# A fused attention and routed feed-forward kernel: the order of the second part's products, its end, and its first fillers

## The chip, the core and the metric

The kernel runs on one core of a Trainium2 chip. The metric is device time in microseconds (us), the median over runs. A core has five engines that run side by side and wait for each other through semaphores: TensorE (PE, matrix products; it writes only to PSUM), VectorE (DVE), ScalarE (ACT), GpSimd (POOL) and SyncE (SP, which issues DMAs; POOL and ACT issue some too). SBUF holds operands, 128 partitions wide; PSUM has eight banks of 512 fp32 values in each partition. In the profile PE has two rows: matmuls, and the loads of their stationary operand (PEld).

## What is computed

Attention first: 8 batches, 8 heads, 512 local and 32 global tokens of width 64, with a band mask for local tokens and full rows for global ones. Its output, 4352 tokens of width 512, goes to a layer of 8 experts whose weights P come from a normalisation repeated eight times over rows and columns:

```python
x = np.ascontiguousarray(attn_out.transpose(0, 2, 1, 3)).reshape(B * S, H * D)
...
for e in range(E):
    h = np.maximum(x @ w1[e], 0.0)      # 4352x512 @ 512x1024
    ye = h @ w2[e]                      # 4352x1024 @ 1024x512
    out += P[:, e:e + 1] * ye
```

Every expert sees every token. The products are by far most of the work.

## The kernel before

The instruction order on each engine is the order in which the Python code emits them (`manual_schedule`); nothing reorders it later. Waits are added where two engines touch the same tile.

The first part computes attention, and beside it experts 0 and 1 in the plain way: `p_l1` makes one 128-row piece of h (four matmuls), `p_l2` one 128-token piece of the output (eight matmuls). What of these is left over when attention ends stands in the list `tail`; some of it runs during the normalisation, and 13 pieces are still there when the second part starts: three long ones (eight matmuls of 512 columns), eight short ones (four of 256 columns), two long ones. The list of short and long ones matters since a long piece needs all short ones before it.

The second part does experts 2 to 7 in two passes over the tokens, with seven products in the place of eight per 2x2 block matrix (a Strassen-like form, whose sums of operands are made by DVE and POOL). Two kinds of objects do it:

- A `Slot`, called a block here, is a 128-wide piece of h for 1024 tokens: products `m1`, `m2`, `m4`, `m6`, `m5`, `m7`, `m3`, each two matmuls of 512 columns (L895; for the 128-column block of the global tokens each is eight matmuls of 128 columns). It works in three PSUM banks: `pa`, `pc` and `pb`. ACT copies `pa` to `pc` after `m1` (L907), takes relu of `pc` after `m2` (L911) and of `pa` after `m4` (L915), and copies `pa` to SBUF after `m6` (L920) and after `m7` (L929). DVE makes the other two quarters of h with a combined add and relu on `pb` (L899): `c22` after `m7`, and another after `m3`. `m4` writes over `pa` once L929 has read it; `m3` adds to `pb` once `c22` has read it.
- A `Unit` is the second layer for 256 tokens: `m1`, `m7`, `m2`, `m6`, `m4`, `m5`, `m3`, each four matmuls of 256 columns (L800), all in one PSUM tile `z` of two banks from the pool `ps_z`, which has two such tiles. ACT copies within `z` after `m1` (L814) and `m6` (L821). DVE (L834; for expert 2 ACT, L839 and L854) reads `z` into the output accumulator three times: `r2` and `r7` after `m5`, `r1` after `m3`. `sums` (L796) are the four operand sums that DVE makes for a unit.

`run_slot(a, jobs)` weaves them. In one call are at hand the new block `a`, the block of the call before `p`, the unit of the call before `x`, and a new unit `y` from a list. `a.m3`, `a.m4` are left to the next call, and so are `m4`, `m5`, `m3` of `y`. `jobs` are loads of the next weights, token sums, and additions of stored results of experts 0 and 1 (`stored_add`, DVE, L755; loads on SP, L747). In the first calls there is no unit yet and `fill` puts leftover pieces between the products; they take the `z` tiles of `ps_z`.

After the last call, `run_slot(None)` finishes the last block and unit, and `plain` does the last four units as plain products: per 128 tokens eight matmuls of 512 columns (L866) into a `z` tile, then one DVE addition (L869) and a store on SP.

Calls are slots in what follows; there are 102 of them, the first beginning at 363.6 us.

Of the kernel before, what the change touches and what calls it, by code (L numbers as in the profile page):

```python
# [23 lines left out]
def kernel(  # L24
# [28 lines left out]
    FT = F // P  # L53
# [636 lines left out]
    with tc.tile_pool(name="tpool", bufs=2) as tpool, \  # L690
# [68 lines left out]
        def store(m, c, eng):  # L759
            if m < B:  # L760
                r0 = S * m + Sg + P * c
                eng.dma_start(out=out[r0 : r0 + P, :], in_=ogs[m][:, c, :])
            else:
                for b in range(4 * c, 4 * c + 4):
                    eng.dma_start(out=out[S * b : S * b + Sg, :], in_=ogs[m][W * (b % 4) : W * (b % 4 + 1), c, :])
# [15 lines left out]
        class Unit:  # L781
# [21 lines left out]
            def w(self, i, j):  # L803
                return w2s[self.k][:, HF * i : HF * (i + 1), H2 * j : H2 * (j + 1)]
# [52 lines left out]
                if self.e == E - 1:  # L857
                    store(self.m, self.c[0], nc.sync)

        def plain(u, last):  # L860
            order = sorted(range(FT), key=lambda fk: (fk % HF == HF - 1, fk))
            for j in range(2):
                for d0, d1 in ((0, H2), (H2, 3 * P), (3 * P, D)) if last and j else ((0, D),):
                    z = ps_mm.tile([P, D], FP32, tag="mm", name="zq") if d0 else ps_z.tile([P, D], FP32, tag="z", name="zp")
                    for n, fk in enumerate(order):
                        nc.tensor.matmul(z[:, d0:d1], u.a[2 * j + fk // HF][:, fk % HF, :], work["last"][:, fk, d0:d1],  # L866
                                         start=(n == 0), stop=(n == FT - 1), skip_group_check=True)
                    o = u.o(j)[:, d0:d1]
                    nc.vector.scalar_tensor_tensor(out=o, in0=z[:, d0:d1], scalar=u.p[j], in1=o, op0=ALU.mult, op1=ALU.add)  # L869
                store(u.m, u.c[j], nc.sync)  # L870
# [67 lines left out]
        units, state = [], dict(slot=None, unit=None)  # L938

        def run_slot(a, jobs=()):  # L940
            p, x = state["slot"], state["unit"]
            y = units.pop(0) if units else None

            def do(who, *what):
                for w in what:
                    if who is not None:
                        getattr(who, w)()

            def fill(n):
                for _ in range(min(n, len(tail)) if a is not None else 0):  # L950
                    tail.pop(0)[1](pool=ps_z, tag="z")

            do(a, "m1")
            some = -(-len(tail) // (HF - a.f)) if tail and a is not None else 0
            if x is None:
                fill(1)
            if a is not None and p is None:
                fill(some)
            do(x, "m4", "m5", "r2", "r7")
            if x is None:  # L960
                do(p, "m4", "m3")
            do(a, "m2")
            if x is not None:
                do(p, "m4", "m3")
            do(y, "sums", "m1")
            do(a, "m6")
            do(x, "m3", "r1")
            do(a, "m5")
            if y is None:
                fill(some - 1)  # L970
            do(y, "m7", "m2", "m6")
            do(a, "m7")
            for j in jobs:
                j()
            do(a, "c22")
            state["slot"], state["unit"] = a, y
# [30 lines left out]
        for k, (pas, e) in enumerate(stages):  # L1007
# [3 lines left out]
            n = len(slots)  # L1011
# [24 lines left out]
            for (q, f), js in zip(slots, jobs):  # L1036
                if k == 0 and q == 1 and f == 0:
                    hset.append([hpool.tile([P, FT, 512], FP16, tag="hT", name="hs") for _ in range(2)])
                run_slot(Slot(k, q, f, hset[q % 2] if q < NQ else hg), js)
                if q == NQ or f == HF - 1:  # L1040
                    push(k, q)
        final, units = units, []
        run_slot(None)
        for i, u in enumerate(final):
            plain(u, i == len(final) - 1)


# [28 lines left out]
```

## Time and profile before

| what | us |
|---|---|
| median of 3 runs | 1017.83 (1014.74 to 1019.41) |
| the profiled execution, its own time | 1014.45 |
| its span | 1012.7 |
| PE busy | 994.9 |
| DVE busy | 778.5 |
| ACT busy | 632.9 |
| POOL busy | 300.6 |

The granted TensorE clock has a mean of 0.996. The span runs from the first to the last instruction of the program; the time of the execution lies some 2 us above it. The ends of matmuls are modelled in a profile of this kind, so that rows of PE overlap: for PE the starts are what to read. In a timeline each row is a start, a length, an engine and line, the operation, what it writes and reads, their shapes, how many like it follow each other (x), and in brackets the idle time before it and what ended that. In the chain of waits each row is a start, a length, and what the end of the program hung on then.

### The profile page before, as it was taken

The numbers are of one execution on the slowest core, as the hardware profiler recorded it, in microseconds if no ns is written. First come the engines' busy times: TensorE is split into PE (matmuls) and PEld (weight loads), VectorE is DVE, ScalarE is ACT, GpSimd is POOL, SyncE is SP. The second block draws the span as 40 slices with busy tenths as digits, with TensorE's granted clock in tenths as the row PEclk, the third lists the DMA queues.
The fourth block names the chain that finished last, engine by engine and source line by source line (L and its number), as shares of the span: only waits on it lengthen the run. The fifth ranks groups of instructions, "written<-read, shape, count | busy, mean of one in ns | idle before, by whom it ended". The sixth has DMA issues, their size and how long they took to land.

```text
span 1012.7 us, 22301 instructions
## 1 busy us (share of the span) xinstructions
PE 994.9 (98%) x8788; PEld 644.5 (64%) x8788; DVE 778.5 (77%) x1889; ACT 632.9 (62%) x1342; POOL 300.6 (30%) x366
## 2 busy tenths in 40 slices
PE   7899999999999999999999999999999999999997
PEld 4656566656565555666666666676767676766764
DVE  7866666666664664889999888997889999888885
ACT  5877777777774566765555555557765555555551
POOL 9648877887760112111111111111111111100000
PEclk8999999999999999999999999999999999999999
DMA  9999999999852297554443333565664533123043
GB/s 169 180 165 197 226 220 208 203 194 228 208 150 84 90 254 167 156 146 115 115 115 74 73 73 74 126 196 138 161 149 119 115 75 86 47 66 74 1 105 125
DMA packets 135882, 138.42 MB, mean 137 GB/s; under 512 B 54432, under 2 KB 107872, under 8 KB 133728
## 3 DMA queue, kind: packets, MB, share of 16 engines
q0 software_dynamic: 105696, 87.32, 49.1%
q1 hardware_dynamic: 29520, 49.34, 15.0%
q8 instruction: 69, 1.13, 0.5%
q10 hardware_dynamic: 560, 0.33, 0.1%
q14 instruction: 37, 0.30, 0.1%
HBM read 144.20 MB, written 39.58 MB: 181 GB/s over the span
## 4 chain that ended last, share of the span: by engine, by line
PE 94%; DVE 3%; ACT 1%; issue 1%; DMA 0%; ACTq 0%; DVEq 0%
PE z L800 29%; PE pa L895 17%; PE ph L467 12%; PE py L481 11%; PE pb L895 9%; PE pc L895 5%; PE po L384 2%; PE zp L866 1%; PE sc L331 1%; PE ptw L350 1%; PE pk L299 1%; DVE ms L338 1%; PE po L428 1%; DVE Pl L347 1%; PE tgx L360 1%; PE pq L299 1%
## 5 line engine op out<-in xcount | busy, mean ns | idle before, releaser
L800 PEld LDWEIGHTS <-hs 128*128 128x128 f16 x2264 | 220.7, 98 | 92.8 <-issue 1.1
L800 PE MATMUL z<-w2e,hs 128*128 128x256 f16 x1304 | 195.6, 273 | 0.9 <-DVE oy L834 0.9
L800 PE MATMUL z<-v,hs 128*128 128x256 f16 x960 | 144.0, 273 | 0.0
L467 PE MATMUL ph<-xT,w1e 128*128 128x512 f16 (+1 forms) x576 | 129.6, 367 | 2.1 <-DVE lg L456 1.4
L481 PE MATMUL py<-w2e,hT 128*128 128x512 f16 x544 | 128.2, 379 | 0.4 <-DVE hT L472 0.4
L821 ACT COPY z<-z 128x256 f32<-128x256 f32 x98 | 35.0, 357 | 142.0 <-PE z L800 142.0
L895 PEld LDWEIGHTS <-w1e 128*128 128x128 f16 x960 | 86.5, 97 | 57.5 <-issue 1.3
L895 PE MATMUL pa<-t,s 128*128 128x512 f16 x384 | 114.2, 379 | 0.2 <-ACT s L920 0.2
L716 POOL DMA_DIRECT2D w1e<-in_moe_w_dram x24 | 17.4, 732 | 306.2 <-PE pa L895 229.9
L341 ACT ACTIVATE Pu<-ms,mx 128x160 f16<-128x160 f32 x256 | 92.3, 424 | 22.9 <-DVE mx L338 20.2
L834 DVE SCALAR_TENSOR_TENSOR oy<-z,lg,oy 128x512 f32<-128x512 f32 x128 | 95.8, 749 | 7.4 <-ACT oy L839 5.2
L796 DVE TENSOR_TENSOR hs<-hs 128x512 f16<-128x512 f16 x224 | 94.9, 423 | 8.2
L338 DVE CUSTOM_DVE_ANT_0 ms<-sc,mask 128x160 f32<-128x160 f32 x256 | 69.9, 320 | 36.7 <-PE sc L333 34.5
L899 DVE CUSTOM_DVE_ANT_0 hx<-pb,s 128x512 f16<-128x512 f32 x96 | 65.9, 686 | 40.0 <-ACT s L929 31.8
L716 POOL DMA_DIRECT2D w2e<-in_moe_w_dram x24 | 19.8, 830 | 242.7 <-PE z L800 212.4
L911 ACT ACTIVATE hs<-pc 128x512 f16<-128x512 f32 x96 | 57.2, 596 | 52.7 <-PE pc L895 52.6
L467 PEld LDWEIGHTS <-w1e 128*128 128x128 f16 x576 | 53.9, 98 | 52.6 <-issue 2.9
L899 DVE CUSTOM_DVE_ANT_0 hs<-pb,s 128x512 f16<-128x512 f32 x96 | 65.8, 686 | 27.3 <-ACT s L929 26.9
L895 PEld LDWEIGHTS <-s 128*128 128x128 f16 x720 | 65.6, 98 | 29.9 <-issue 1.8
L481 PEld LDWEIGHTS <-hT 128*128 128x128 f16 x544 | 50.0, 98 | 51.8 <-issue 0.5
L472 DVE TENSOR_SCALAR hT<-ph 128x512 f16<-128x512 f32 x58 | 40.1, 692 | 47.7 <-PE ph L467 46.4
L929 ACT COPY s<-pa 128x512 f32<-128x512 f32 x102 | 59.8, 586 | 12.3 <-PE pa L895 1.1
(196 smaller groups left out, 1971.4 us busy)
## 6 DMA issues: line engine op xcount, KB each, us to landing
ys<-yd SPq DMA_DIRECT2D x68, 256.0 KB, 3.4
yd<-yst SPq DMA_DIRECT2D x16, 1024.0 KB, 5.6
pw<-in_moe_w_dram POOLq DMA_DIRECT2D x24, 512.0 KB, 10.3
kept<-psum POOLq DMA_DIRECT2D x24, 512.0 KB, 4.7
s<-kept POOLq DMA_DIRECT2D x12, 768.0 KB, 9.2
v<-kept POOLq DMA_DIRECT2D x12, 768.0 KB, 8.8
w1e<-in_moe_w_dram POOLq DMA_DIRECT2D x12, 512.0 KB, 5.3
w2e<-in_moe_w_dram POOLq DMA_DIRECT2D x12, 512.0 KB, 6.6
```

Source lines behind the costliest of these rows:

```text
L338: nc.vector.tensor_tensor_reduce(out=ms[:, ii, :], in0=sc[:, SW * ii : SW * (ii + 1)], in1=mask[:, mi, :], scale=-scale, scalar=BIG, op0=A ...
L341: nc.scalar.activation(out=d["Pu"][:, i, :], in_=ms[:, ii, :], func=AF.Exp, scale=-1.0, bias=d["mx"][:, i : i + 1])
L467: nc.tensor.matmul(ph[:, 0:n], wts[e][0][:, dk, P * fm : P * (fm + 1)], xT[:, dk, c0 : c0 + n], start=(dk == 0), stop=(dk == DP - 1))
L472: nc.vector.tensor_scalar(out=hT[:, fm, 0:n], in0=ph[:, 0:n], scalar1=0.0, scalar2=None, op0=ALU.max)
L481: nc.tensor.matmul(py, hT[:, fk, P * c : P * (c + 1)], wts[e][1][:, fk, :], start=(fk == 0), stop=(fk == FT - 1))
L796: nc.vector.tensor_tensor(out=o, in0=x, in1=y, op=op)
L800: nc.tensor.matmul(o, lhs[:, fk, :], rhs[:, fk, :], start=(first and fk == 0), stop=(fk == HF - 1), skip_group_check=True)
L834: nc.vector.scalar_tensor_tensor(out=o, in0=z, scalar=p, in1=o, op0=ALU.mult, op1=ALU.add)
L895: nc.tensor.matmul(o, lhs[:, dk, P * f : P * (f + 1)], rhs[:, dk], start=(first and n == 0 and dk == 0), stop=(dk == HD - 1), skip_group_c ...
L899: nc.vector._custom_dve(TENSOR_ADD_SAT, out=self.to(i, j), in0=self.of(ps), in1=self.of(s), s0=BIG, s1=0.0)
L911: nc.scalar.activation(out=self.to(0, 0), in_=self.of(self.pc), func=AF.Relu)
L929: nc.scalar.copy(out=self.pre3, in_=self.pa)
```

## The change

Three edits.

1. In `run_slot`, the old block's `m4` is emitted right after the old unit's products, ahead of the new block's `m2`; it stood between the new block's `m2` and the old block's `m3`. (Where there is no old unit, `m4` and `m3` both stood ahead of `m2`, and still do.)
2. In the first slot, two leftover pieces stand between `m1` and `m2` in place of five, and the count for the rest of the slot is lowered by one. Over the four slots that have pieces, their numbers go from 8, 2, 2, 1 to 4, 3, 3, 3.
3. `run_slot(None)` is written out: the last unit's `m4`, `m5`, `r2`, then the last block's `m4`, `m3`, then `r7`. The last unit's `m3` and `r1` are handed to `plain`, which emits them after six of the eight matmuls of its first product.

```diff
-        def plain(u, last):
+        def plain(u, last, between=()):
             order = sorted(range(FT), key=lambda fk: (fk % HF == HF - 1, fk))
...
                     for n, fk in enumerate(order):
+                        if n == FT - 2 and j == 0:
+                            for f in between:
+                                f()
                         nc.tensor.matmul(z[:, d0:d1], u.a[2 * j + fk // HF][:, fk % HF, :], work["last"][:, fk, d0:d1],
...
             if x is None:
                 fill(1)
             if a is not None and p is None:
-                fill(some)
+                fill(1)
+                some -= 1
             do(x, "m4", "m5", "r2", "r7")
+            do(p, "m4")
             if x is None:
-                do(p, "m4", "m3")
+                do(p, "m3")
             do(a, "m2")
             if x is not None:
-                do(p, "m4", "m3")
+                do(p, "m3")
...
         final, units = units, []
-        run_slot(None)
+        p, x = state["slot"], state["unit"]
+        for w in (x.m4, x.m5, x.r2, p.m4, p.m3, x.r7):
+            w()
         for i, u in enumerate(final):
-            plain(u, i == len(final) - 1)
+            plain(u, i == len(final) - 1, (x.m3, x.r1) if i == 0 else ())
```

## The prediction

> **What bounds the kernel now.** I read the page first, then the busy time by stretch, the chain of waits, and the timeline of one steady slot, of the first slots and of the end.
>
> ```profile
> span 1012.7 us, 22301 instructions
> PE 994.9 (98%) x8788; PEld 644.5 (64%) x8788; DVE 778.5 (77%) x1889; ACT 632.9 (62%) x1342; POOL 300.6 (30%) x366
> ```
> ```profile
> 500.00:550.00 50.00, 50.00 (x344) 33.38 (x342) 46.26 (x82) 28.14 (x57) 5.66 (x8) 1.00 0.47 112
> ```
>
> TensorE (PE) sets the pace; in this stretch of the second part it is busy 50.00 of 50.00 us at a granted clock of 1.00, VectorE (DVE) 46.26, ScalarE (ACT) 28.14. But a PE row's length is not the time it takes from its successor: in the timeline below, two matmuls last 0.59 and the next pair starts 0.43 later. A stall shorter than that overlap is invisible as idle time, so I go by starts.
>
> ```profile
> 984.35 0.59 PE L895 MATMUL pa<-t,s 128*128 128x512 f16 x2
> 984.78 0.59 PE L895 MATMUL pa<-xT,w1e 128*128 128x512 f16 x2
> 985.22 0.60 PE L800 MATMUL z<-v,hx 128*128 128x256 f16 x4
> 985.65 0.60 PE L800 MATMUL z<-w2e,hx 128*128 128x256 f16 x4
> 986.16 0.59 PE L895 MATMUL pc<-xT,w1e 128*128 128x512 f16 x2
> 986.59 0.59 PE L895 MATMUL pa<-t,w1e 128*128 128x512 f16 x2
> 987.02 0.59 PE L895 MATMUL pb<-xT,s 128*128 128x512 f16 x2
> 987.46 0.60 PE L800 MATMUL z<-w2e,hs 128*128 128x256 f16 x4
> 987.89 0.59 PE L895 MATMUL pa<-t,s 128*128 128x512 f16 x2
> 988.32 0.60 PE L800 MATMUL z<-w2e,hs 128*128 128x256 f16 x4
> 988.76 0.59 PE L895 MATMUL pb<-xT,w1e 128*128 128x512 f16 x2
> ```
> ```profile
> 985.04 0.59 ACT L929 COPY s<-pa 128x512 f32<-128x512 f32 x1
> 985.52 0.59 ACT L907 COPY pc<-pa 128x512 f32<-128x512 f32 x1
> ```
> ```profile
> 985.66 0.69 DVE L899 CUSTOM_DVE_ANT_0 hs<-pb,s 128x512 f16<-128x512 f32 x1 [1.01 <-ACT s L929]
> 986.29 1.54 DVE L834 SCALAR_TENSOR_TENSOR oy<-z,lg,oy 128x512 f32<-128x512 f32 x2
> 987.74 0.68 DVE L899 CUSTOM_DVE_ANT_0 hs<-pb,s 128x512 f16<-128x512 f32 x1
> ```
>
> This is a slot, PE's rows first, then ACT's and DVE's: old block's m7 at 984.35, new block's m1 at 984.78, old unit's m4 and m5 at 985.22 and 985.65, new block's m2 at 986.16, old block's m4 and m3 at 986.59 and 987.02. Products follow each other after 0.43 to 0.44, except m2: 0.51 after m5. It waits for the copy of pa into pc (L907), which ends at 985.52 + 0.59 = 986.11; 0.05 later m2 starts. The copy is late because it stands behind L929, the copy of m7.
>
> ```profile
> 451.45 0.45 PE pc L895 x2
> ...
> 457.54 0.50 PE pc L895 x2
> ```
> ```profile
> 405.74 1.31 PE z L800 x12
> ...
> 989.36 1.31 PE z L800 x12
> ```
>
> The chain of waits shows the same as 0.50 (elsewhere 0.45) for a pair that takes 0.43. Between the two z rows lie 95 slots in 583.62 us, 6.143 each. A slot at full rate is 28 matmuls of 256 columns at 1.31/12 = 0.1092 and 14 of 512 at 0.2156 (the mean spacing of the unstalled ones), 6.075; times 95 is 577.1, and the six slots of the 128-column block take some 0.6 more. That leaves 5.9 us of stall. Counted start by start, 62 slots lose 0.075, five 0.060, 27 lose 0.020 and one 0.369: 5.89, all ahead of m2.
>
> [...] Taken instead at its word, the busy row of 50.00 would leave nothing to win in this stretch and the sum below would be 0.9 us.
>
> **Part 1, old block's m4 ahead of new block's m2.** Nothing is added on any engine; PE's order becomes m1, m4, m5 (unit), m4 (block), m2, m3. Take m7 as zero. The block's m4 would start at 1.74 (985.22 + 2 × 0.435 - 984.35). It overwrites pa, so it needs L929, which ends at 985.63, or 1.28 (1.32 with the handover): 0.4 to spare. m2 comes at 2.17 and needs L907, ready at 1.81: 0.36 to spare. So the stall goes. What is late next: m3 of the old block needs c22 (the DVE row at 985.66, ending 986.35, 2.00), and would come at 2.60. The new block's m5 needs pb's last reading (987.74 + 0.68 = 988.42, 4.07) and would come at 4.34 instead of 4.41: the least margin, 0.2. The sums for the new unit's m7, which follows m5, stand behind that same DVE row, the first ending 0.42 or so after it: some 0.3 to spare. ACT reads pa before pc instead of after; pc's relu ends some 0.4 later, and the next use of its output is a slot away. If a cover fails, its late part costs up to 95 × 0.075 again. The DVE needs 46.26/50 × 6.15 = 5.69 a slot, under 6.08, so it doesn't become the pace. Gain taken: 5.9; bounds 0 (another wait takes the place everywhere) and 5.9 (no more stall than this).
>
> The moved product's first matmul now carries a wait on ACT of its own (m2's wait, on a later copy, covered it before): 99 more waits in the built program. The unit's m4 (985.22) carries such a wait too, on an ACT copy that is done by then, and starts 0.44 after its predecessor. I take nothing; the bounds are 0 and, by the one handover that shows (986.11 to 986.16), 0.05 each, 5 us.
>
> **Part 2, leftover pieces spread.**
>
> ```profile
> 370.31 0.60 PE L467 MATMUL ph<-xT,w1e 128*128 128x256 f16 x4 [0.24 <-ACT yst L484]
> ```
> ```profile
> 379.16 0.59 PE L895 MATMUL pa<-t,w1e 128*128 128x512 f16 x2
> 379.86 0.38 PE L895 MATMUL pb<-xT,s 128*128 128x512 f16 x1
> ```
> ```profile
> 387.27 0.59 PE L895 MATMUL pa<-t,s 128*128 128x512 f16 x2
> 387.79 0.59 PE L895 MATMUL pb<-xT,w1e 128*128 128x512 f16 x2
> 388.60 0.38 PE L895 MATMUL pa<-t,s 128*128 128x512 f16 x1 [0.22 <-ACT s L920]
> ```
> ```profile
> 379.62 1.45 POOL L716 DMA_DIRECT2D w1e<-in_moe_w_dram  x2 [21.10 <-PE ph L467]
> ```
>
> Thirteen pieces fill four slots: before 8, 2, 2, 1, after 4, 3, 3, 3; none is added. By starts this region loses 2.1 us. Two short pieces behind three long ones wait for their bank (0.40 and 0.20); after, one short piece follows one long one and the rest come two by two with m7 and m1 between, so these 0.6 go. In the fourth slot m7 waits for its pa copy at 388.60: 0.81 after m5 instead of 0.43, 0.38 lost; after, two long pieces stand there, and it goes. But the fourth slot had a long piece between m1 and m4 that hid c22; now a short one stands there as in the third, where m3 came 0.70 after m4 (379.86 against 379.16), 0.27 lost: that is new. Some 1.1 of waits of 0.08 to 0.3 in the four slots and the first of the units stays. Gain 0.98 - 0.27 = 0.7; bounds 0 and 1.0.
>
> The next weights on POOL's queue (379.62) wait for the last short piece, which moves from the third slot to the fourth, some 3 us later. They are read from the next stage on, four slots of 6.1 after the fourth, so they have over 20 us. The store of the last leftover group goes out a few us later on SP, behind the same loads as before; the accumulator that takes its buffer is first written three slots on. I cost both at nothing; without that cover each would cost its delay, 2 to 4 us once.
>
> **Part 3, the end.**
>
> ```profile
> 992.55 0.59 PE L895 MATMUL pb<-xT,s 128*128 128x512 f16 x2
> 994.00 0.60 PE L800 MATMUL z<-w2e,hs 128*128 128x256 f16 x4 [0.85 <-DVE oy L834]
> 994.43 0.81 PE L866 MATMUL zp<-w2e,hs 128*128 128x512 f16 x3
> ```
> ```profile
> 991.81 0.69 DVE L899 CUSTOM_DVE_ANT_0 hs<-pb,s 128x512 f16<-128x512 f32 x1 [1.01 <-ACT s L929]
> 992.41 1.53 DVE L834 SCALAR_TENSOR_TENSOR oy<-z,lg,oy 128x512 f32<-128x512 f32 x2
> 993.86 0.68 DVE L899 CUSTOM_DVE_ANT_0 hs<-pb,s 128x512 f16<-128x512 f32 x1
> 994.63 0.75 DVE L834 SCALAR_TENSOR_TENSOR oy<-z,lg,oy 128x512 f32<-128x512 f32 x1
> ```
>
> The unit's m3 starts 1.45 after the block's m3, whose pair takes 0.43: 1.01 lost behind both readings (r2, r7) of 992.41 to 993.94. After, six plain matmuls (6 × 0.216 = 1.30) start at 992.98 and end at 994.28. The block's relu sum now stands between r2 and r7, and moves r7's end to about 992.41 + 0.75 + 0.68 + 0.75 - overlaps = 994.55, so m3 starts at 994.6, not 994.28. Then its reading r1 (0.63 after m3's start, 0.75 long) ends at 995.98. The second plain product writes the bank pair that r1 frees, and only 2 × 0.216 of plain work follows m3 (ends 995.46): a new wait of about 0.55. That product starts at 996.0; before, at 994.43 + 8 × 0.216 = 996.16. So of 1.0 won, 0.15 is left; bounds -0.3 (r1 half a read later) and 0.5 (m3 needs r2 alone). Stores on SP keep their order.
>
> **Sum.** 5.9 + 0.7 + 0.15 = 6.75. The profiled execution took 1014.45 around a span of 1012.7; less 6.75 it is 1007.7. It is 3.4 below the median of the runs shown, 1017.83, near their lowest, 1014.74. Taken from the median the forecast is 1011.1, which I give.
>
> **Rivals.** *A, another wait takes the place (no change).* The nearest is the new block's m5 on pb, with 0.2 to spare. For: 46.26 of 50 on DVE. Against: in the quoted slot it idles 1.01 before c22, and every margin above exceeds the 0.075 that the order shifts. If it does, 0.9 is left: 1017.
>
> *B, the new wait itself costs (slower).* At 5.89/99 = 0.06 each it eats the steady gain; slower by half a per cent from (6.75 + 5.1)/99 = 0.12 each, where the time would be 1023. Against stands the unit's m4 at 985.22. [...]
>
> *C, part of it stays.* Where two stored additions and the DVE's other work fill a slot, c22 starts late and m3, with 0.6 to spare here, takes over the wait. If half of the 95 slots keep their stall, 2.9 less is won: 1014.0.
>
> **Chances.** Forecast 0.72, A 0.10, B 0.06, C 0.12. Half a per cent, 5.1 us, is about what a measurement here can tell from no change (the three runs span 1014.74 to 1019.41); the forecast's 6.75 is near it, so of its 0.72 some 0.05 falls inside, and C and A do. Faster 0.67, same 0.27, slower 0.06. The range goes from 1005.5 (all bounds won, and a run like the profiled one) to 1017 (A).
>
> **What would show it.** Steady slots of 6.08 from z row to z row; m2's pair 0.43 after block m4, both without a gap; DVE's idle time before c22 shorter by 0.07. In the first slots no wait of m7 on L920's copy, and one more of m3 on c22. At the end unit m3 among plain products near 0.3 late and a new wait of the second plain product on r1. Wrong would be slots still at 6.14 with the gap ahead of m4, m3 or m5, or a gap ahead of every m4 whose release had long come.

## The result, and the profile after

The changed kernel takes 1008.74 us (median of 6 runs, 1007.68 to 1011.77); the kernel before took 1016.29 over six runs by now (1013.49 to 1019.79). The ratio is 0.9933, with a 95% interval of 0.9906 to 0.9959. It is faster by about 0.7%, as forecast; the forecast of 1011.1 hung on the first three runs of before, whose median was 1.5 us higher. The medians lie 7.55 apart, and the stretches that the edits touch account for 6.37 of it (below). The rest is within the spread of the runs, so that the ratio comes so near the forecast's is in part chance.

The page of the changed kernel:

```profile
span 1005.9 us, 22302 instructions
PE 989.4 (98%) x8788; PEld 645.4 (64%) x8788; DVE 778.6 (77%) x1889; ACT 632.9 (63%) x1342; POOL 300.7 (30%) x366
```

PE is still at 98% of the span, and DVE and ACT do what they did. The row of busy time says nothing of where the time went. The starts do. One steady slot, PE's timeline (start, length, engine, line, operation, tiles, count):

```profile
978.26 0.59 PE L898 MATMUL pa<-t,s 128*128 128x512 f16 x2
978.69 0.59 PE L898 MATMUL pa<-xT,w1e 128*128 128x512 f16 x2
979.12 0.60 PE L800 MATMUL z<-v,hx 128*128 128x256 f16 x4
979.56 0.60 PE L800 MATMUL z<-w2e,hx 128*128 128x256 f16 x4
979.99 0.59 PE L898 MATMUL pa<-t,w1e 128*128 128x512 f16 x2
980.42 0.59 PE L898 MATMUL pc<-xT,w1e 128*128 128x512 f16 x2
```

The same slot on ACT, and on DVE:

```profile
978.94 0.59 ACT L932 COPY s<-pa 128x512 f32<-128x512 f32 x1
979.43 0.59 ACT L910 COPY pc<-pa 128x512 f32<-128x512 f32 x1
980.62 0.60 ACT L918 ACTIVATE hs<-pa 128x512 f16<-128x512 f32 x1 [0.61 <-PE pa L898]
981.12 0.59 ACT L914 ACTIVATE hs<-pc 128x512 f16<-128x512 f32 x1
```
```profile
979.56 0.69 DVE L902 CUSTOM_DVE_ANT_0 hs<-pb,s 128x512 f16<-128x512 f32 x1 [0.94 <-ACT s L932]
980.20 1.54 DVE L834 SCALAR_TENSOR_TENSOR oy<-z,lg,oy 128x512 f32<-128x512 f32 x2
```

The old block's m4 starts 0.43 after the unit's m5, and the new block's m2 0.43 after that; no product waits. The copy that m2 needs (L910, L907 before) ends at 980.02, 0.40 ahead of m2. The idle time of DVE before c22 went from 1.01 to 0.94, by the 0.07 that each slot lost in length. (Lines stand three lower in the changed file.) The chain of waits, first and last full group of unit products in the steady slots:

```profile
405.12 1.31 PE z L800 x12
...
977.11 1.31 PE z L800 x12
```

Here 94 slots take 571.99 us, 6.085 each, against 6.143 before; without the 0.6 of the narrow block's slots it is 6.078, which is 28 matmuls at 0.1092 and 14 at 0.2158, and nothing else.

The start of the first unit's slot, where waits remain, on PE:

```profile
387.94 0.59 PE L898 MATMUL pa<-t,s 128*128 128x512 f16 x2
388.37 0.59 PE L898 MATMUL pa<-xT,w1e 128*128 128x512 f16 x2
388.80 0.38 PE L909 MATMUL pc<-xT,identity 128*128 128x512 f16 x1
389.26 0.59 PE L898 MATMUL pa<-t,w1e 128*128 128x512 f16 x2
389.99 0.59 PE L898 MATMUL pb<-xT,s 128*128 128x512 f16 x2
```

m3 comes 0.73 after m4 instead of 0.43. In the fourth slot, where a long piece had hidden c22, it is now the same, 0.69:

```profile
381.99 0.59 PE L898 MATMUL pa<-t,w1e 128*128 128x512 f16 x2
382.68 0.59 PE L898 MATMUL pb<-xT,s 128*128 128x512 f16 x2
```

The end, PE and then DVE:

```profile
986.38 0.59 PE L898 MATMUL pb<-xT,s 128*128 128x512 f16 x2
986.82 1.46 PE L869 MATMUL zp<-w2e,hs 128*128 128x512 f16 x6
988.42 0.60 PE L800 MATMUL z<-w2e,hs 128*128 128x256 f16 x4
988.85 0.59 PE L869 MATMUL zp<-w2e,hs 128*128 128x512 f16 x2
989.86 0.38 PE L869 MATMUL zp<-w2e,hs 128*128 128x512 f16 x1 [0.41 <-DVE oy L834]
```
```profile
985.64 0.69 DVE L902 CUSTOM_DVE_ANT_0 hs<-pb,s 128x512 f16<-128x512 f32 x1 [0.94 <-ACT s L932]
986.25 0.74 DVE L834 SCALAR_TENSOR_TENSOR oy<-z,lg,oy 128x512 f32<-128x512 f32 x1
987.01 0.69 DVE L902 CUSTOM_DVE_ANT_0 hs<-pb,s 128x512 f16<-128x512 f32 x1
987.62 0.74 DVE L834 SCALAR_TENSOR_TENSOR oy<-z,lg,oy 128x512 f32<-128x512 f32 x1
989.05 0.75 DVE L834 SCALAR_TENSOR_TENSOR oy<-z,lg,oy 128x512 f32<-128x512 f32 x1 [0.69 <-PE z L800]
```

Six plain matmuls stand ahead of the unit's m3, which still waits for r7 (987.62 + 0.74, then 0.06): 0.31. Then the second plain product waits at 989.86 for r1: 0.57.

### The profile page after: what moved, and what is told of

Read it like the earlier page. It is cut to its first block, busy times and chain, and to the rows that moved or that the text cites. A ratio compares the mean times of both kernels' runs of the same rounds, so it can differ in the third digit from the quotient of the medians.

```text
span 1005.9 us, 22302 instructions
## 1 busy us (share of the span) xinstructions
PE 989.4 (98%) x8788; PEld 645.4 (64%) x8788; DVE 778.6 (77%) x1889; ACT 632.9 (63%) x1342; POOL 300.7 (30%) x366
## 4 chain that ended last, share of the span: by engine, by line
PE 95%; DVE 3%; ACT 1%; issue 0%; DVEq 0%; ACTq 0%
PE z L800 30%; PE pa L898 17%; PE py L481 12%; PE ph L467 12%; PE pb L898 9%; PE pc L898 4%; PE po L384 2%; PE ptw L350 1%; PE sc L331 1%; PE zp L869 1%; PE pk L299 1%; DVE ms L338 1%; PE po L428 1%; PE tgx L360 1%; PE pq L299 1%; ACT Pu L341 0%
## 5 line engine op out<-in xcount | busy, mean ns | idle before, releaser
L341 ACT ACTIVATE Pu<-ms,mx 128x160 f16<-128x160 f32 x256 | 92.4, 424 | 22.3 <-DVE mx L338 19.6
L834 DVE SCALAR_TENSOR_TENSOR oy<-z,lg,oy 128x512 f32<-128x512 f32 x128 | 95.8, 748 | 8.0 <-ACT oy L839 5.2
L796 DVE TENSOR_TENSOR hs<-hs 128x512 f16<-128x512 f16 x224 | 94.9, 423 | 8.2
L918 ACT ACTIVATE hs<-pa 128x512 f16<-128x512 f32 x96 | 57.2, 596 | 46.8 <-PE pa L898 46.7
L120 POOL TENSOR_TENSOR psum<-pw 128x512 f16<-128x512 f16 x48 | 55.1, 1181 | 45.6 <-DMA pw<-in_moe_w_dram 45.6
```

What stands on the lines that cost most here:

```text
L120: nc.gpsimd.tensor_tensor(out=o, in0=x, in1=y, op=op)
L341: nc.scalar.activation(out=d["Pu"][:, i, :], in_=ms[:, ii, :], func=AF.Exp, scale=-1.0, bias=d["mx"][:, i : i + 1])
L796: nc.vector.tensor_tensor(out=o, in0=x, in1=y, op=op)
L834: nc.vector.scalar_tensor_tensor(out=o, in0=z, scalar=p, in1=o, op0=ALU.mult, op1=ALU.add)
L918: nc.scalar.activation(out=self.to(1, 0), in_=self.of(self.pa), func=AF.Relu)
```

## The experiments

The starts of five instructions cut every trace into the same stretches: the first product of a block; the first unit's first product (its L811); the m7 of the last block; the second plain product; the last plain matmul.

| kernel | start to first block product | first slots | steady slots | end | plain products |
|---|---|---|---|---|---|
| before | 363.64 | 27.81 | 599.06 | 5.65 | 12.07 |
| changed | 363.70 | 27.14 | 593.49 | 5.52 | 12.07 |
| part 1 alone | 366.61 | 27.80 | 593.50 | 5.65 | 12.07 |
| part 2 alone | 365.24 | 27.15 | 599.08 | 5.65 | 12.07 |
| part 3 alone | 368.37 | 27.81 | 599.06 | 5.52 | 12.07 |
| m4 one product earlier | 369.38 | 27.14 | 614.35 | 5.52 | 12.07 |
| the same without r7 | 364.28 | 27.15 | 594.77 | 5.52 | 12.07 |
| m4 two products earlier | 365.78 | 27.14 | 654.75 | 5.52 | 12.07 |
| m3 ahead of m2 too | 368.76 | 27.14 | 593.49 | 5.52 | 12.07 |
| second plain product in another bank | 365.49 | 27.14 | 593.49 | 4.95 | 12.07 |
| changed, with three more edits and the other bank | 366.25 | 26.49 | 593.49 | 4.79 | 12.07 |

From the first block product to the last plain matmul, what an edit doesn't touch repeats within 0.02 us. The first column, which no edit touches, spreads over 5.7 us. So one profile of each kernel settles a tenth of a microsecond in a stretch, where whole times differ by several for no reason of the edit.

**Part 1 alone.**

```diff
-            if x is None:
-                do(p, "m4", "m3")
+            do(p, "m4")
+            if x is None:
+                do(p, "m3")
             do(a, "m2")
             if x is not None:
-                do(p, "m4", "m3")
+                do(p, "m3")
```

> Part 1 alone (block m4 ahead of the new block's m2; first slots and end as before). Theory: the stall of m2 is the whole steady gain. From the first unit's first product to the last block's m7 the kernel before takes 599.1 us; here 593.2 to 593.5, with no gap ahead of m4, m2, m3 or m5. The first slots (first block product to first unit product) stay at 27.8, the end (last m7 to second plain product) at 5.65. Time 5.6 to 5.9 us below before, ratio 0.9945. Rival A (another wait takes the place): 599 in the steady stretch. Rival C: about 596.

The steady slots took 593.50, the rest was as before. By time the ratio is 0.9935 (0.9912 to 0.9958), 1010.71 us against 1016.18. The gain of the steady slots is all this edit's, and nothing took the wait's place.

**Part 2 alone.**

```diff
             if a is not None and p is None:
-                fill(some)
+                fill(1)
+                some -= 1
```

> Part 2 alone (leftover pieces 4, 3, 3, 3 instead of 8, 2, 2, 1). Theory: the first slots take 27.1 us instead of 27.8: no wait of pieces for their bank, none of m7 on the copy of pa in the fourth slot, one more wait of m3 on c22 (0.27). Steady stretch 599, end 5.65 as before. Rival: the pieces' waits come back in other slots, first slots at 27.8.

First slots 27.15, the rest as before: 0.66 won.

**Part 3 alone** (the hunks on `plain` and on the end of the change).

> Part 3 alone (last unit's m3 among the first plain product). Theory: the 1.01 wait of the unit's m3 falls to 0.3, a new wait of 0.55 to 0.6 stands ahead of the second plain product, and the end takes 5.5 us instead of 5.65. Steady stretch 599.1, first slots 27.8. Rival (the second plain product waits for nothing): end at 4.9.

End 5.52: 0.13 won, where the wait that was removed had cost 1.01. The three parts add up: 5.56 + 0.66 + 0.13 = 6.35, and the whole change moved these stretches by 6.37.

**The second plain product in another bank**, which asks whether its wait is for the bank alone.

```diff
-                    z = ps_mm.tile([P, D], FP32, tag="mm", name="zq") if d0 else ps_z.tile(...)
+                    z = ps_mm.tile([P, D], FP32, tag="mm", name="zq") if d0 or (between and j) else ps_z.tile(...)
```

> The changed kernel with the second plain product in a bank of the other pool, nothing else. Theory: its wait on r1 (0.57) goes, the end takes 4.95 us in place of 5.52; the unit's m3 still waits 0.31 behind r7. Rival: the second plain product waits at the same time for something else, or loses it at the third product; the last PE instruction then comes no earlier.

End 4.95, and the plain products behind it are no longer: the 0.57 was the bank, and stays won.

**m4 two products earlier**, and **one product earlier**, which ask what releases m4.

```diff
-            do(x, "m4", "m5", "r2", "r7")
-            do(p, "m4")
+            do(p, "m4")
+            do(x, "m4", "m5", "r2", "r7")
```

> The changed kernel with the block's m4 two products earlier, straight after the new block's m1. Theory: m4 would come 0.87 us after m7 and waits until 1.32 (1.26 in some 20 slots, earlier in the narrow block's six): 0.45, 0.40 and 0.25 lost, about 41 us over the steady stretch, 593.5 + 41 = 634 to 635. m2 then loses nothing. Rival (PE is held by something else than that copy): no more than a few us, since the same products run.

```diff
-            do(x, "m4", "m5", "r2", "r7")
-            do(p, "m4")
+            do(x, "m4")
+            do(p, "m4")
+            do(x, "m5", "r2", "r7")
```

> The changed kernel with the block's m4 one product earlier, between the unit's m4 and m5. Theory: m4 is released by the copy of the old block's m7 (L929 before, here L932), done with handover 1.32 us after m7 in most slots and 1.26 in some 20. m4 would come at 1.30: a wait of 0.02 in some 70 slots, steady stretch 593.5 to 595 us. Rival (the added wait itself costs, wherever it stands, or a later event releases it): 0.1 or more a slot, over 600.

Two earlier, PE's timeline around m4:

```profile
798.47 0.59 PE L898 MATMUL pa<-t,s 128*128 128x512 f16 x2
798.90 0.59 PE L898 MATMUL pa<-xT,w1e 128*128 128x512 f16 x2
799.79 0.59 PE L898 MATMUL pa<-t,w1e 128*128 128x512 f16 x2 [0.30 <-ACT s L932]
```

m4 starts 1.32 after m7, exactly at its expected release. Counted by starts, m4's wait sums to 42.5 us over the steady slots where 41 was expected, and one product earlier to 1.5, 0.02 in 64 slots, as expected too. But both lost some 19 us more than m4's own wait: 61.3 in all in place of 41, and 20.9 in place of at most 1.5. The extra is on none of the products that were moved. One product earlier, the chain of waits shows groups of unit products that are longer than their 0.44 and 1.31:

```profile
800.60 0.49 PE z L800 x4
801.09 0.43 PE pb L898 x2
801.52 1.43 PE z L800 x12
```

By starts the unit's m7 loses 0.095 a slot, m3 0.057, m6 0.035 (9.2, 5.3 and 3.4 us), all released by DVE (sums L796, reading L834), and another 2.0 us lie in hundredths behind those. DVE's own timeline, c22 and then r2 and r7:

```profile
804.10 0.69 DVE L902 CUSTOM_DVE_ANT_0 hx<-pb,s 128x512 f16<-128x512 f32 x1
805.18 1.54 DVE L834 SCALAR_TENSOR_TENSOR o<-z,lg,o 128x512 f32<-128x512 f32 x2 [0.40 <-PE z L800]
```

In the changed kernel r2 follows c22 with no gap; here DVE stands idle 0.40 until the unit's m5 is done, which the moved m4 delays by a product. Everything behind r2 in DVE's order comes later by as much. That was left out of the expectation. It is so in most slots: the idle time before r2 has a median of 0.40 us here and 0.83 with m4 two products earlier, where it is 0 in the changed kernel. Whether this chain is the whole of it was asked by taking r7 out of the chain, which leaves that term out of the output:

```diff
-            do(x, "m5", "r2", "r7")
+            do(x, "m5", "r2", "s7")     # s7: r7's store alone
```

> The kernel with m4 one product earlier (between the unit's m4 and m5) took 614.35 us in the steady stretch where 593.5 to 595 was expected; m4 itself lost only some 0.02 a slot. Here the same order, but DVE's second reading r7 of each unit is left out (that term is missing in the output; its store stays). Theory: the loss is DVE's chain. r2 waits for the unit's m5, which the moved product delays by 0.43, and r7, the sums and the next readings stand behind it. With 0.7 less in that chain the unit's m3, m7 and m6 wait for nothing, and only m4's 0.02 is left: steady stretch 595 us. Rival (m4's place costs PE itself, through its wait or its bank): 610 or more.

Steady slots 594.77. All waits on DVE went; by starts 1.5 us is left at m4 and nothing else. DVE still idles 0.39 before r2 in most slots, so that delay alone costs PE nothing: it reached PE because r7 and the rest of the chain stand behind it. So the place of the product costs what its own release costs, and the other 19.6 us (614.35 less 594.77) came through DVE.

**m3 ahead of m2 too**, for the margin that is left on c22.

```diff
             do(p, "m4")
-            if x is None:
-                do(p, "m3")
+            do(p, "m3")
             do(a, "m2")
-            if x is not None:
-                do(p, "m3")
```

> The changed kernel with the old block's m3 ahead of the new block's m2 as well. Theory: m3 comes 2.17 us after m7 and needs c22, whose end with handover stands at 2.05 in most slots and 2.16 in the worst one in the changed kernel's trace: no wait, steady stretch 593.5 within 0.5; m2 has still more room. The margin that part 1 left is then 0.1. Rival C (c22 is late where DVE is full): waits of 0.1 or more in many slots, 596 or above.

593.49, with no wait in any steady slot: c22 is never later than 2.17 after m7, so m3 had over 0.43 to spare where the change left it.

**Three more edits, with the other bank as above**: r7 back ahead of the block's m4 and m3, the unit's m3 after four plain matmuls, and two pieces between m1 and m4 in the slots before there are units. (The bank's line of the diff stands above.)

```diff
-                        if n == FT - 2 and j == 0:
+                        if n == FT - 4 and j == 0:
...
-            if a is not None and p is None:
+            if a is not None and x is None and tail:
                 fill(1)
                 some -= 1
...
-        for w in (x.m4, x.m5, x.r2, p.m4, p.m3, x.r7):
+        for w in (x.m4, x.m5, x.r2, x.r7, p.m4, p.m3):
```

> The changed kernel with three more edits: r7 ahead of the block's m4 and m3, unit m3 after four plain matmuls in place of six, the second plain product into a bank of the other pool, and in slots two to four two leftover pieces between m1 and m4 in place of one. Theory: end 4.8 us in place of 5.5 (r7 at its old place lets m3 start some 3.5 after m7, no bank to wait for); first slots 26.5 in place of 27.1 (c22 done before m3 comes, 2.05 after m7 against 2.17); steady stretch as in the changed kernel, 593.5. 1.3 to 1.4 us below the changed kernel, ratio to before 0.992. Rival (the two waits at the end are one chain, and r1 is only late elsewhere): end at 5.5.

Its end on PE:

```profile
988.28 0.59 PE L898 MATMUL pb<-xT,s 128*128 128x512 f16 x2
988.72 1.02 PE L869 MATMUL zp<-w2e,hs 128*128 128x512 f16 x4
989.73 0.60 PE L800 MATMUL z<-w2e,hs 128*128 128x256 f16 x4
990.16 0.59 PE L869 MATMUL zp<-w2e,hs 128*128 128x512 f16 x2
```

m3 follows four plain matmuls with 0.15 lost in place of 0.31, and the next product waits for nothing. First slots 26.49, end 4.79: 1.38 us less than the changed kernel in these stretches, as worked out. By time 1006.87 us (6 runs), a ratio to before of 0.991 (0.9891 to 0.993): the fastest of all, though its lead over the changed kernel is read from the stretches, not from times, which overlap.

## Why the prediction was right

- *What bounds.* Right: PE's starts, not its busy time. In the slot of the changed kernel above, m4's row lasts 0.59 and m2 starts 0.43 after it. Going by the busy row of 50.00 in 50.00 nothing was to be won in the stretch that gave 5.57 us.
- *Part 1*, taken as 5.9, measured 5.57. The mechanism holds: m4's release was put at 1.32 after m7, and with m4 moved up to meet it, it starts at 1.32; m2's stall went in every slot, and the 99 new waits, all of which the trace records, 97 of them at an m4 in the steady slots, cost nothing, since a slot is now the sum of its matmuls. The size of the term was too large by 0.33. I took a full-rate slot as 6.075, with 0.2156 a matmul of 512 columns, a mean over a trace full of short stalls. Undisturbed it is 0.2158 and the slot 6.078: in the kernel before, the first four such matmuls behind each stall of 0.075 ran at 0.2150, so some 0.003 of every stall came back.
- *Part 2*, 0.7, measured 0.67. The two bank waits and m7's wait on the copy went, the new wait on c22 came (0.26 at 382.68). What stays by starts is 1.44 us, against the 1.1 and the new 0.27 of the working: m4 in the first unit's slot lost 0.05 more, now that the last long piece's copy (L484, at 388.14) stands ahead on ACT of the copy of m7 (L932, at 388.62 with no idle time before it; before, ACT idled 0.68 there).
- *Part 3*, 0.15, measured 0.13. Both waits came where they were put: m3 lost 0.31 (0.3) behind r7, which the relu sum pushed back, and the second plain product 0.57 (0.55) behind r1.
- *The sum*, 6.75. The stretches moved by 6.37. The profiled spans differ by 6.75 all the same, because the last store landed 0.45 sooner after the last plain matmul (4.00 against 4.45) and the first part ended 0.06 later; that agreement is chance.
- *Rivals.* A and C are out: part 1 alone won all of it, and even m3 ahead of m2 meets no wait. B is out by the slot's length, 6.078 against the 6.14 of before: at each of the 97 m4 in the steady slots the wait is on an ACT copy that is done by then, and m4 starts 0.436 to 0.437 after the unit's m5, which is that product's four matmuls at 0.1092 and nothing more.
- *Margins.* The least margin of the prediction, and with it the nearest form of A, was the new block's m5, 0.2 behind pb's last reading. That wait is not there in 97 of the 98 steady slots: from the second on, the traces record for m5 a wait on ACT and none on DVE. With m4 one product earlier, m5 starts 0.11 before that reading ends in 96 of them. One is this:

```profile
668.16 0.68 DVE L902 CUSTOM_DVE_ANT_0 hs<-pb,s 128x512 f16<-128x512 f32 x1
668.73 0.59 PE L898 MATMUL pb<-xT,w1e 128*128 128x512 f16 x2
```

  So the prediction's sum was safe from this danger for another reason than the one it gave. The margin of the unit's m7 on DVE's sums, worked out as 0.3, is borne out: in the changed kernel m7 starts 0.36 after its first sum ends (median; 0.24 in 13 slots), and with DVE's chain some 0.4 later it lost 0.1. The unit's m3, for which no margin was worked out, starts 0.42 after r7 ends (median), and lost 0.06 then.

## What to carry to other kernels

Where one engine looks full, subtract starts: one stall of 75 ns or less in nearly every slot did not show as idle time, and without them the kernel is 0.55% shorter. A product can be moved into such a gap when its own release has come (m4's came 1.32 after m7, and it starts 1.74 after m7 now), but look also at what it delays: m4 one place earlier had met its release and still lost 19 us, because a reading on another engine, with a full chain behind it, hung on the product that was pushed back. And a wait of 1.01 at the end gave 0.13: 0.31 of it stayed, and a new one of 0.57, for a bank to be freed, stood just behind it.

## What the runs showed that was not expected

The first part of this kernel ended at 363.6 to 369.4 us in eleven traces of a part that no edit touched, while 27, 594 and 12 us behind it repeated within 0.02. Most of the spread of the profiled spans, beyond what the edits do, is that of the first part; the last store adds 3.9 to 4.5 us after the last plain matmul. The spread of the first part builds up all along: its 601st matmul starts at 39.7 to 43.9 us, and from there to the first block product it takes 322.4 to 325.7. What varies there stays open.
